# Nine of the sixteen input tiles come transposed from HBM instead of through TensorE, with a new list of operations

## The chip, the cores and the metric

The kernel runs on one core of one Trainium2 chip. The metric is the time of one execution on the device in microseconds (us); the lower the better. The kernel before takes 492.57 us, the median of three runs (491.83 to 493.06).

## The reference, cut to what matters

The input x has 2048 rows (tokens) of 512 numbers. It is normalised by rows, then goes through two branches, whose results are multiplied and added to x.

```python
x = A_x                                     # 1 x 2048 x 512
xn = _layernorm(x, axis=-1)                 # (x - mean) / sqrt(var + 1e-5), row by row
s = _A_ref(xn, A_wqkv, A_w_phi, A_wo)       # linear attention, 32 heads of 16
g = _silu(_B_ref(xn, B_w1, B_b1, B_w2))     # dense 512 -> 1792, mish, dense 1792 -> 512
return x + s * g

# in _A_ref: qkv = x @ wqkv; q and k go through w_phi and two softmaxes each;
# kv = phi_k^T v and z = sum of phi_k over all tokens; o = phi_q kv / (phi_q z); o @ wo
```

## The kernel before, in words

The 2048 tokens are 16 tiles of 128 tokens (`NT`), numbered 0 to 15. Every matrix product on TensorE needs the normalised x transposed: features on the partitions, tokens along the row. In the kernel that is `xT`, one tile of 128 x 2 x 4 x 128 for each 128 tokens: the first half (called high) is the value rounded to the fast matmul type fp32r, the second half (low) is what the rounding left. Each product then takes three matmuls (low by high, high by low, high by high), which `mm3` and `kv_product` issue.

The function `norm` (operation `N` in the list `ORDER`) makes one tile of `xT`. It loads the tile of x with tokens on the partitions (`load_x`), takes mean and variance by BN_STATS and BN_AGGR on VectorE (`mv`), computes one over the deviation (an addition on VectorE, a power on GpSimd, `rs`) and minus mean by that (`nb`), normalises the tile in one pass with these as scalars of each partition (on VectorE or ScalarE), and lets TensorE transpose it by four matmuls with the identity into a bank of PSUM (`pt`). `split` copies the bank out twice: ScalarE writes the high half, VectorE the low one. Then the tile goes to HBM (`scr`) for the second branch.

The products use Strassen's scheme with seven products in place of eight, so sums and differences of pairs of tiles are needed, here tile t and tile t + 4. `sums_x` makes them (`ts`, and split `th` and `tl`) from the two banks `pt`: since an instruction of GpSimd can't read PSUM here, it first copies one of the banks to SBUF (`xr`). They go to HBM too (`scrT`).

After that come, for the attention: products for k and v (`kv_a` to `kv_d`, banks `kx`, `ky`, `kz`), for q (`q_proj`, bank `q`, stored to HBM as `qd` from a copy `qs` and loaded again), two softmaxes each (`k_soft`, `q_soft`), the sums over all tokens (`kv_acc`, bank `kvp`; `sums`), denominators (`den`) and a transposition of each q tile in blocks into `ph0` (tiles 0 to 7) or `ph1` (8 to 15), the products with kv (`num`, banks `pn`, which need all eight tiles of `ph0` or `ph1`) and with wo (`att_out`). For the other branch: `ffn1a` to `ffn1d` (banks `fx`, `fy`, `fz`), the activation Mish, `ffn2` and `ffn2a` to `ffn2d`. `final` takes SiLU, multiplies by the attention's result and adds x, and stores.

No scheduler runs at build time that would decide the order. Every operation is recorded by `Program`, and a table of numbers, `SCHED`, says in which order the recorded operations are issued, and by a letter behind a number on which of two engines an operation runs where both could do it (V is VectorE, G GpSimd, A ScalarE). A second table, `PLACE`, gives each tile its place in the pools: 38 slots, 15 small slots `s2`, the banks of PSUM and some more. Each engine takes its instructions strictly in the order of the list, so an instruction that waits holds all that stand behind it on its engine. All DMAs but the very first are issued from SyncE (SP), also in order. Since all operations are issued by one helper, nearly all instructions have line 182 in the profile.

Of the kernel before, what the change touches and what calls it, by code (L numbers as in the profile page):

```python
# [10 lines left out]
F32 = mybir.dt.float32  # L11
# [19 lines left out]
PLAIN = (0,)  # L31
# [18 lines left out]
232A 275 236 380 233 193 210 92 325 183 110V 308 37 237 211 158 238 64 178 360 111G 220 184A 239 194 118A 125V 188G  # L50
179 167 195A 180 240A 276 361 168 427 212 93 112 259 196 391 213 241 169V 277 221 200A 381 362 146G 326 197 245A 214
327 65 278 127 309 279A 119 198 166 215A 201 223 246 242 260V 222A 247G 224 328 202V 428 310 203V 329 392 280 311 128A
249 429 330 227 243 284A 312 147 248V 225V 216 228A 254 285 319G 217 561 287V 84 161 382 113 255 286G 293 256A 363 288
331A 257 364 313 199 295 320 314V 218 281 393 162V 394 315 250 332 261 114 316 599 94 321G 159 294A 204 148 333 430
305 395 181 317 289 282 263 251V 306A 383 365A 396V 229 115G 322 307 262V 350 264 384 265 340 266 296 336 318 297 226
341 299G 252 366 185 342 337 267G 205 323A 268G 355 370A 351A 371 344V 431A 372G 352 298 367 338A 290V 300G 432 269
356 368 270 369 397 219 422 139 398 373V 374 401A 399 385A 324 436A 353A 357V 386 301 400 95V 459 358 207 437 387 170
334 420 438G 354 206G 375 388 410 440 423A 343 421A 404V 457 302 345G 474 402 376G 208 346 411 244 271 253 458A 507
335 460 412 519 461 403V 414V 472 405 413 447 462 415G 473A 303 475 463G 416 445 600V 272G 520A 439V 484 508A 477 441
389 347 377 525 339 602G 446V 464G 348 485 442V 349G 469 486A 448 465 476 509 417 433 406 478G 378 424 487 470A 407G  # L60
488 526A 505 471 466 495 489G 449 450 304G 522 496 408 291 510 521 451V 498 452G 549 497 527 490G 573 467 479V 491
562V 551 566 499V 564G 512 523A 651 539 500V 409 601G 292 434 501 492 468G 532 511 553 533A 493 513G 480 418 419V 591
494G 550A 552A 540 453 524 481 574 482 603G 565V 514G 611 542 575A 558 541 577 612A 543V 567V 578 544V 559V 693 506A
560 639 515 435 454 570G 572 545 638 637 455 528 579A 534 516 563G 640 618 685 456G 647 517 712 529 546 483G 502 581
646 530A 547 635 503 548G 582 571V 621 650 283 518G 649 535 583 613 536 531 504V 580 614 593V 576 622 594V 595 652V
584 598 623A 654V 713 636A 624 610 604 596V 443 554 605V 625 585V 656 653V 698 597V 615 537A 586V 555 657V 824 587
608V 568 645 620 648 643 556A 609G 616A 619V 557 680 854 714 538 588 444 660 655G 699V 606 569G 682 617 681A 661A 663
662 626 687 678 694G 658 686 664A 668 688G 679V 696G 707 607G 644 592V 665 669 589 627 709 689G 628 695V 702 715V 629V
641 716V 727 630G 642 671 717 666 720 697G 708A 659V 667 728A 778 722 721A 590V 700 739 631 683 701G 710 723 632 704
750G 792 724A 703V 684 690 633 670 733 725 672G 718 726 729 711 821 634V 736 673V 751G 756 730 674 734V 705 735 675  # L70
706 743 793G 731V 732 822 744A 676 691 677G 746 757 753V 752 747A 740A 759V 755 754G 834 856 829 766 831 741 780 767
797V 719 828 771 779 995 768A 764V 832 823 786 765V 745 692 802 781G 758 774 787A 748 788 769 742 849 830 803G 775 770
737 843 855 850A 794G 804 806 760G 846 807A 799 844V 782G 795 798 845 872 800 805V 801 796V 808 789 873A 888 835V 783
827 813G 749 862 790 833 761 836 777 867 863A 762 738 772A 837G 904 942 814 773 933 1037 905A 815V 816 817 877V 818G
874 838 784 819G 851 791 776 878 916 857G 847 896V 826 906 858G 986 763 885 897 879G 785 864 907 886A 852 859 880 898V
959 899 820 868A 917A 839 869 889 960A 840G 841G 865 920 900 918 881 919 875 923 882G 866 1039 853 876 901V 860 922
825 908G 912 902G 921A 861 1003 934A 997 924A 890 929 870 910G 977 943 925 883G 842 887 930A 1100 991 931 955 909V 932
992V 871 936 884 956A 913G 939 926 940 987G 811 903 1093 911G 941 963 961 891V 914 1089 935 962 1102 892G 809 937A 996
964A 1122 1006 944 988G 893 989V 927 982 950 915V 1087 928 1016 965 945V 978V 1099 946G 951V 810 952 848 957 983G 990V
1011 979G 966 1007 993 953 980G 1009 954 994V 981G 958 1045 967 1018 1088 1010A 969V 1017A 998G 1029 1101 970 1012  # L80
999G 1030A 1086 971V 1034 972 1013A 973 1019 1000 1014 1020 1031 968 1047 1008 974V 1123 938 975G 1032 1090 984 1001
947 1166 1097 1002 1021G 976 1053 1038 985V 1108 1054A 1033A 1055 1078G 1064 1109A 1022 1057 894 1065A 1094 1015 1046
1067 1058A 1040G 1096 1035 812 1004A 1079 1059 1041G 895 1095 1042 1060 1066 1048G 1133V 1023G 1114 1124 1125G 1484
1147 948 1080G 1049V 1164 1148A 1024 1115A 1025 1081 1043 1111 1103G 1165A 1185 1036 1061A 1050 1026G 1062 1141 1126G
1068 1027G 1051 1176 1092 1142A 1098 1167 1005 1149 1134 1082 1169 1112 1083G 1150 1119 1044 1151 1170A 1084V 1248
1135G 1144 1130 1104V 1056 1091 1028 1105 1172 1070G 1339 1177A 1085 1121 1173A 1127 1136 1145 1171 1249 1071 1190
1052 1137 1120A 1274 1072G 1138V 1073 1168 1174 1116 1139G 1220 1074 1357 1131 1191V 1152 1128 1485 1250 1140 1182
1340 1075V 1117 1076G 1179 1183 1106 1178 1180A 1257G 1153A 1181 1118 1197 1192 1194 1251 1154 1175 1143 1186 1107
1063 1132V 1358 1214 1200 1293 1198 1201 1188 1366 1156G 1204 1228 1392 1215A 1205 1155 1199 1276 1202 1193 1217 1208
949 1187G 1203 1445 1206 1225 1218 1252G 1195 1518 1207 1209 1146 1231 1229 1212 1226A 1157 1439 1359 1189G 1360 1275  # L90
1375 1254 1234 1235 1277G 1232 1238 1367 1255 1239 1216 1196G 1242 1221 1243 1459 1233 1253 1246 1258 1236 1320 1210
1278G 1256 1213 1247 1237 1158G 1227 1259V 1240 1341V 1265 1223 1260 1295 1279 1261 1159 1211 1262G 1224G 1077 1328
1266A 1241 1361G 1368 1129 1280 1281 1446 1268 1312G 1475 1377 1342 1321 1369 1294 1421 1343G 1313 1244 1344 1245
1222G 1334 1314V 1069 1407 1263V 1352 1362 1491 1269A 1345A 1323V 1346 1282V 1365 1430 1230 1296V 1301 1322 1270 1297V
1324G 1315 1160 1325 1290 1316 1161V 1317V 1162V 1335V 1298 1163 1363 1460 1355 1461 1408 1364 1356G 1264 1318G 1331
1326 1302A 1447 1303 1283 1395 1423 1370V 1409 1284G 1271 1336V 1304G 1353 1416 1113 1376 1291A 1371 1272V 1378 1292
1354V 1329A 1373 1396V 1330 1285 1452 1393 1605 1372 1410 1379V 1533 1432 1299 1374 1422 1419 1286 1383 1332A 1411V
1420G 1382 1454 1417 1287V 1402 1394V 1380 1288G 1431 1305 1337 1486 1381 1300 1497 1333 1306G 1273 1413 1307 1289
1424 1611 1219 1448 1184 1338V 1414 1110 1308 1477 1309V 1425V 1403 1415 1327 1405 1428 1476 1406V 1404V 1412 1418V
1433 1310V 1499 1426 1434G 1453 1384V 1498 1429 1478 1427 1479V 1436 1347 1802 1385 1440 1438 1519 1492 1311 1386G  # L100
1539 1435 1524 1449G 1441 1387 1480 1535 1520 1388 1482 1455 1389V 1319 1390G 1437 1462G 1391 1451 1463G 1442V 1450
# [93 lines left out]
def block_kernel(ctx: ExitStack, tc: tile.TileContext, x, xt, wqkT, wv, phi, wo, w1, b1, w2, out):  # L195
# [14 lines left out]
    def alloc(tag, shape, name, dtype=F32):  # L210
        return pools[tag].tile(shape, dtype, tag=tag + next(places), name=name)
# [687 lines left out]
```

## Time and profile before

| | |
|---|---|
| time, median of three runs | 492.57 us (491.83 to 493.06) |
| the profiled execution's own time | 492.47 us |
| its span (first to last instruction) | 490.7 us |
| mean granted clock of TensorE | 0.996 |
| transposes of x tiles on TensorE | 64, four for each tile |
| HBM traffic | 72.92 MB read, 42.07 MB written |

The profile is of one execution. PE is TensorE's matmul queue, PEld its loads of weights (they overlap), DVE is VectorE, ACT ScalarE, POOL GpSimd, SP SyncE and SPq its queue of DMA issues. A row of grouped instructions reads: line, engine, operation, names out<-in with buffer numbers left out, shapes, count; then busy time and mean duration in ns; then the idle time of the engine just before these instructions and what ended it. A row of waits reads: who waited <- for whom: us in total, times, longest. A row of a timeline reads: start, us from start to end, engine, line, operation, names, shapes, count.

### The profile page before, as it was taken

Reading aid. Unit: us, or ns where it says so; the run is one execution under the profiler, and the core shown is the slowest. Engines: PE = TensorE matmul, PEld = TensorE weight load, DVE = VectorE, ACT = ScalarE, POOL = GpSimd, SP = SyncE. Lnnn points to the kernel's source line nnn. Section 1 sums busy time; section 2 is a strip of 40 time slices with the busy share of each in tenths; the row PEclk is TensorE's granted clock in tenths of the full one; section 3 lists DMA queues with packets and bytes.
Section 4 is the critical chain, followed back from the end, with each engine's and each line's share of the span. In section 5 each row is a group of like instructions: output and inputs, shape, how many; then the busy total and the mean of one; then the engine's idle time right before and its main releaser. Section 6 shows DMA issues by size and latency. Waiting matters only on the chain.

```text
span 490.7 us, 8536 instructions
## 1 busy us (share of the span) xinstructions
PE 482.5 (98%) x3126; PEld 397.9 (81%) x3126; DVE 428.0 (87%) x658; ACT 270.1 (55%) x408; POOL 276.8 (56%) x204
## 2 busy tenths in 40 slices
PE   9999999999999999999999999999999999999994
PEld 9888888888888788887888778888888887888883
DVE  5998989999989998989999978979956699889974
ACT  4777754544071524333434778587496487657721
POOL 2889556986548657567575687353642334612440
PEclk9999999999999999999999999999999999999998
DMA  8736838344977689979788896867686652484366
GB/s 296 286 123 243 303 126 338 152 133 120 375 253 265 207 289 342 287 258 298 264 268 286 319 351 233 278 196 234 214 288 230 211 193 67 152 276 154 107 203 203
DMA packets 65592, 115.53 MB, mean 235 GB/s; under 512 B 7056, under 2 KB 32016, under 8 KB 65552
## 3 DMA queue, kind: packets, MB, share of 16 engines
q1 hardware_dynamic: 65408, 114.75, 68.6%
q8 instruction: 24, 0.39, 0.3%
q10 hardware_dynamic: 144, 0.26, 0.1%
q14 instruction: 16, 0.13, 0.1%
HBM read 72.92 MB, written 42.07 MB: 234 GB/s over the span
## 4 chain that ended last, share of the span: by engine, by line
PE 94%; DVE 3%; issue 1%; DMA 1%; POOL 0%; SPq 0%; ACT 0%; DVEq 0%; ACTq 0%
PE y L182 19%; PE fx L182 14%; PE q L182 9%; PE pw L182 9%; PE kx L182 8%; PE fy L182 8%; PE x L182 6%; PE ky L182 4%; PE fz L182 3%; PE pn L182 2%; PE kz L182 2%; PE z L182 2%; PE kvp L182 2%; PE pt L182 1%; PE k L182 1%; PE v L182 1%
## 5 line engine op out<-in xcount | busy, mean ns | idle before, releaser
L182 PE MATMUL q<-wqh,xT 128*128 128x512 f32 x128 | 43.0, 395 | 0.0
L182 ACT ACTIVATE r<-r,b1t 128x512 f32<-128x512 f32 x56 | 37.9, 715 | 3.0 <-DMA r<-hd 3.0
L182 PEld LDWEIGHTS q<-wqh,xT 128*128 128x128 f32 x128 | 24.0, 188 | 5.1
L182 PE MATMUL q<-wql,xT 128*128 128x512 f32 x64 | 25.0, 390 | 0.0
L182 DVE TENSOR_REDUCE tz<-ez 128x64 f32<-128x1024 f32 x16 | 19.3, 1204 | 1.3 <-POOL ez L182 1.3
L182 ACT ACTIVATE hb<-fx 128x512 f32<-128x512 f32 x13 | 7.5, 593 | 18.4 <-PE fx L182 18.4
L182 PE MATMUL kx<-wss,th 128*128 128x512 f32 x56 | 17.3, 390 | 0.0
L182 POOL TENSOR_TENSOR w2t<-w2t 128x256 f32<-128x256 f32 (+1 forms) x4 | 6.0, 1496 | 19.7 <-DVE w2t L182 12.9
L182 ACT ACTIVATE qs<-q 128x512 f32<-128x512 f32 x12 | 6.9, 595 | 17.9 <-PE kvp L182 10.0
L182 POOL TENSOR_TENSOR rs<-rs,mhalf 128x1 f32<-128x1 f32 x16 | 9.8, 620 | 12.0 <-DVE rs L182 11.3
L182 DVE TENSOR_TENSOR ol<-pn,oh 128x256 fp32r<-128x256 f32 x32 | 12.1, 415 | 4.9 <-ACT oh L182 4.9
L182 ACT ACTIVATE hc<-fx 128x512 f32<-128x512 f32 x13 | 7.7, 598 | 15.0 <-PE fx L182 15.0
L182 ACT ACT_TABLE_LOAD x12 | 15.4, 1283 | 0.2
L182 ACT ACTIVATE w1sh<-w1s 128x1024 fp32r<-128x1024 f32 x7 | 7.4, 1059 | 11.8 <-DVE w1s L182 6.2
L182 PEld LDWEIGHTS q<-wql,xT 128*128 128x128 f32 x64 | 12.0, 188 | 2.3
L182 DVE BATCH_NORM_STATS2 st<-x 128x6 f32<-128x512 f32 x16 | 10.7, 682 | 3.6 <-DMA x<-x 3.6
L182 POOL TENSOR_TENSOR w<-w2r,w 128x512 fp32r<-128x512 f32 x7 | 9.0, 1295 | 8.5 <-ACT w L182 8.5
L182 DVE TENSOR_TENSOR xT<-pt,xT 128x512 fp32r<-128x512 f32 x16 | 10.8, 680 | 2.0 <-ACT xT L182 1.2
L182 PE MATMUL pw<-oh,wo0l 128*128 128x512 f32 x32 | 12.5, 390 | 0.0
L182 PE MATMUL pw<-ol,wo0h 128*128 128x512 f32 x32 | 12.5, 389 | 0.0
L182 PE MATMUL pw<-oh,wo0h 128*128 128x512 f32 x32 | 12.5, 389 | 0.0
L182 PE MATMUL pw<-oh,wo1l 128*128 128x512 f32 x32 | 12.4, 389 | 0.0
(862 smaller groups left out, 1864.3 us busy)
## 6 DMA issues: line engine op xcount, KB each, us to landing
r<-hd SPq DMA_DIRECT2D x28, 512.0 KB, 5.3
qd<-qs SPq DMA_DIRECT2D x16, 256.0 KB, 6.3
scr<-xT SPq DMA_DIRECT2D x8, 512.0 KB, 5.3
scrT<-th SPq DMA_DIRECT2D x8, 512.0 KB, 4.6
scrT<-tl SPq DMA_DIRECT2D x8, 512.0 KB, 5.4
qp<-qd SPq DMA_DIRECT2D x16, 256.0 KB, 5.8
xx<-xt SPq DMA_DIRECT2D x16, 256.0 KB, 4.9
so<-so SPq DMA_DIRECT2D x16, 256.0 KB, 3.1
```

The source lines that it names most:

```text
L182: getattr(g, m)(*a, **k)
```

## The change

For the nine tiles in `TURNED` the host's transposed copy of x (`xt`, which `final` reads already) takes the place of the transposition on TensorE. The mean and the deviation of each token are computed as before from the tile with tokens on the partitions, which is still loaded. But now they are needed along the row, the same on all partitions. So the pair `mv` of each partition is written to HBM as two rows of 128 numbers (`row`, one number from each partition), and loaded back to all 128 partitions (`bc`). The transposed tile is loaded from `xt` (`nx`), the mean is subtracted and the product with one over the deviation taken, in two passes over 128x512 on VectorE or GpSimd. `nx` takes the place of `pt` behind that: in SBUF, so that its low half and its sums may also be made on GpSimd, and no copy `xr` is needed where the second tile of a pair is turned.

`norm_turned` is new, `norm` branches to it, the end of `norm` becomes `keep_x`, and `sums_x` takes either kind:

```diff
+TURNED = (3, 6, 7, 9, 10, 11, 13, 14, 15)
...
+    def norm_turned(t, mv):
+        rs = mv[:, 1:2]
+        V.tensor_scalar(rs, rs, 1e-5, None, op0=ALU.add)
+        G.tensor_tensor(rs, rs, mhalf, op=ALU.pow)
+        row = dram.tile([2, P], F32, name=f"row{t}")
+        Q.dma_start(row.rearrange("c p -> p c"), mv)
+        bc = alloc("s2", [P, 2, P], f"bc{t}")
+        Q.dma_start(bc.rearrange("p c n -> p (c n)"), row.rearrange("c n -> (c n)").partition_broadcast(P))
+        nx = alloc("s2", [P, KC, P], f"nx{t}")
+        Q.dma_start(nx, xt.rearrange("(k p) n -> p k n", p=P)[:, :, t * P:(t + 1) * P])
+        for c, op in ((0, ALU.subtract), (1, ALU.mult)):
+            either(nx, nx, bc[:, None, c, :].to_broadcast([P, KC, P]), op=op)
+        return nx
...
         V.bn_aggr(mv, st)
+        if t in TURNED:
+            w = slot([P, 2, KC, P], f"xT{t}", F32R)
+            pt = norm_turned(t, mv)
+            split(pt, w[:, 0], w[:, 1], either)
+            return keep_x(t, w, pt)
...
-        xr = s2(f"xr{t}")
-        copy(xr, p2.rearrange("p k n -> p (k n)"))
-        xr = xr.rearrange("p (k n) -> p k n", k=KC)
+        xr = p2
+        if p2.space == "PSUM":
+            xr = s2(f"xr{t}")
+            copy(xr, p2.rearrange("p k n -> p (k n)"))
+            xr = xr.rearrange("p (k n) -> p k n", k=KC)
+        first = V.tensor_tensor if p1.space == "PSUM" else either
...
-        V.tensor_tensor(ts[:, 0], xr[:, 0:2], p1[:, 0:2], op=ALU.subtract)
+        first(ts[:, 0], xr[:, 0:2], p1[:, 0:2], op=ALU.subtract)
```

`SCHED` and `PLACE` are replaced as a whole by other numbers; the list `ORDER`, by which the operations are recorded, stays as it is. The first line of `SCHED`:

```diff
-27 16 0 13 1 46 2 19 3 15 4 74 5 17 28 6 96 7 14 18 8 123 9 29 10 30 47 20 11 31 12 42 129 48 32 49 33V 50 120 21 51
+27 13 0 74 1 96 2 16 3 46 4 15 5 17 28 6 18 7 14 123 8 120 29 9 30 75 10 149 31 11 12 76 98 32 276 33V 129 47 42 99 48
```

What this does to the queues is shown at three places. The first is TensorE just ahead of the first product with tile 3 (bank `kx3`, from the high half of the k weights `wkh` and `xT3`). Before:

```order
L182 MATMUL kz2_309<-wkh1_176,xT2_231 128x512
L182 MATMUL kz2_309<-wkl1_177,xT2_231 128x512
L182 MATMUL kz2_309<-wkh1_176,xT2_231 128x512 x2
L182 MATMUL kz2_309<-wkl1_177,xT2_231 128x512
L182 MATMUL kz2_309<-wkh1_176,xT2_231 128x512
L182 MATMUL pt9_322<-ident_83,x9_316 128x128 x4
L182 MATMUL pt10_332<-ident_83,x10_326 128x128 x4
L182 MATMUL kx3_290<-wkh0_160,xT3_265 128x512
```

And in the changed kernel at the same place:

```order
L183 MATMUL v4_269<-wv1h_212,xT4_168 128x512
L183 MATMUL v4_269<-wv1l_213,xT4_168 128x512
L183 MATMUL v4_269<-wv1h_212,xT4_168 128x512 x2
L183 MATMUL v4_269<-wv1l_213,xT4_168 128x512
L183 MATMUL v4_269<-wv1h_212,xT4_168 128x512
L183 MATMUL kx3_289<-wkh0_160,xT3_264 128x512
```

The transposes of tiles 9 and 10 are gone, as are those of 3, 6 and 7 further ahead; products of tiles 4 and 8 stand there that came later before, and a product of tile 2 (`kz2`) comes behind.

The second place is SP's list of DMAs around the pair of rows of tile 3: `row3` is its write to HBM, `bc3` its load to all partitions. In the changed kernel (`scr` and `scrT` are stores of finished tiles, `qd1` is the store of tile 1 of q, `nx11` the transposed load of tile 11):

```order
L183 DMA qd1_109<-qs1_274 128x512
L183 DMA row9_318<-mv9_316 128x2x1
L183 DMA bc6_281<-row6_280 128x256
L183 DMA row3_265<-mv3_263 128x2x1
L183 DMA nx11_357<-xt 128x4x128
L183 DMA scr1_103<-xT5_220 128x2x256
L183 DMA scrT0_106<-tl0_174 128x1024
L183 DMA bc7_301<-row7_300 128x256
L183 DMA x14_358<-x 128x512
L183 DMA bc3_266<-row3_265 128x256
L183 DMA qd2_110<-qs2_238 128x512
```

Before, at the rows with these numbers, stand stores alone, the last of which is that of tile 12 of q:

```order
L182 DMA scrT0_106<-tl0_174 128x1024
L182 DMA qd4_112<-qs4_206 128x512
L182 DMA qd0_108<-qs0_236 128x512
L182 DMA scrT0_106<-th1_225 128x1024
L182 DMA w1a2_449<-w1 128x1024
L182 DMA scr0_102<-xT1_184 128x1024
L182 DMA qd12_120<-qs12_287 128x512
```

The loads of nine rows and nine transposed tiles now stand among these stores, and those of q come later.

The third place is VectorE around the transposition of tile 7 of q into `ph0`, the last that `num` needs. Before:

```order
L182 SCALAR_TENSOR_TENSOR den8_726<-tz8_725 128x32
L182 TENSOR_TENSOR hc6_784<-hc6_784,fy6_782 128x512
L182 RECIPROCAL den8_726<-den8_726 128x32
L182 COPY hc5_792<-fx5_769 128x512
L182 TENSOR_REDUCE q13s_761<-q13e_760 128x64
L182 STREAM_TRANSPOSE ph0_584<-q7e_710 128x32x32
```

In the changed kernel:

```order
L183 STREAM_TRANSPOSE ph0_579<-q6e_627 128x32x32
L183 TENSOR_REDUCE q11m_831<-qp11_829 128x32
L183 TENSOR_TENSOR q7e_705<-q7e_705,q7r_703 128x1024
L183 TENSOR_TENSOR hb6_778<-hb6_778,fy6_777 128x512
L183 STREAM_TRANSPOSE ph0_579<-q7e_705 128x32x32
L183 TENSOR_REDUCE tz8_720<-ez8_719 128x64
```

The scaling of `q7e` is now done by VectorE itself, two places ahead of its transposition, and the steps of the denominator of tile 8 have moved behind.

More of the change, by code (lines that the diff above doesn't have):

```diff
@@ L50 @@
[L50 to L59, printed above, removed]
@@ new lines @@
+196 282 165A 229 370 244G 180 200A 201 439 245G 390 93 168 230A 197 440 161 325V 225 441 169A 401 263V 215 112 127
+284G 170 166 202V 319 226 198 251V 371 203V 309 249 318 285G 217V 147 119 257 84 250V 218G 338 204 442 402 258 337
+162V 219 372 320G 205 472 252 391 220V 326 207 321G 297 408 253 113 148 246 223 392 254V 227A 322 128A 264 403 323V
+298A 247V 299 289V 265A 373 339V 290G 664 248 266 300 228 340G 301 231 292G 267 303G 341 114 404 259A 302 328 405 268
+304G 406 327V 344 255 329A 260 291G 310A 185 363 269 94 293 270G 407 364 311 181 393 305 271V 159 360 375V 272 294V
@@ new lines @@
+553 429 587 464G 356 484 452G 590 588A 505 613G 454 589 421 578G 508 448V 357G 554 536A 562 524 479 545 565A 455V 651
+518 465V 491G 509 591 571 526V 492V 537 527G 592A 506 466 593 307 456 624 480 507G 546A 296 467 493 400 548 563A 556V
+308G 510 604 494 549 605A 511 615G 457 614V 512G 631 430 555 659 616G 495 573 513V 576G 547 632A 585 572V 519A 625A
+566 528 557V 663 725 580V 594 514 583V 558 567 431V 581 584G 648 529 634 515 595 665G 656 635 652 559 606G 657 541
+636A 597 516 626 627 667G 481V 517G 568 847 650 468 413 560 628 596 530 561V 542 843 496V 608 543A 653 617 607V 611
@@ new lines @@
+669 623 550A 670V 629A 638 569A 609V 649A 698 570 531V 673 707V 658 619 720 469V 630 551 674A 660 610V 691 637 544 711
+633 618V 805 692A 449 621V 598G 695 726 693 712V 708G 639 676 694A 599V 709G 696 722 677A 675 668G 697 600 661 699
+728G 717 640 721A 622V 678 666V 836 727 620G 681 723 641 715 582V 662 769 729G 733 716A 679 671 682 680 740 834 701G
+700 734A 724 684 710G 736 672V 741A 642G 713 752 601 702G 743 683 753A 714V 737A 742 703 643V 685G 758 644 754 718
+744A 756 602 719 686V 755 603G 645 687 746 654 770 735 646 747A 763V 757A 647G 748 835 759 791 688 745 764V 765 655
@@ new lines @@
+1042 916 1046A 950A 983 1024 951 998G 1043A 1013 966 1025 1060 967 1014 1091G 1066 1026A 1137 1027 1070 1067A 1288
+1028 984G 1034G 822 1092 1077 1071A 1114 1073 907 958G 1106 1103 957 1160 941 1074A 908 1452 959G 1035 1109 1154 824
+1261 1015 985 1179 1036G 1155V 1078A 1053G 960 986 987V 1072 1037 988G 961 1127 1048 1110 1068 1093G 1121 1075 1038
+1076 1054V 1039G 1069 1177 1094 1055 823 1061G 989 1079 1157 1178A 1138V 1128A 1180 1124 1062V 1146V 1063 1129 1161A
+1125 1083G 1105 1262 1111 1056 1080 1130 1132 1122A 1147 1104 1139G 1112 1126 1064 1040G 1199 1182 1181 1133A 1263
@@ new lines @@
+1057 1162 1065 1183A 1095 1041 1189 1370 1116G 1148V 1131 1264 1096G 1185 1149 1200G 1163 1233 1388 1097V 1184 1117G
+1186A 1140 1192 1187 1158 1165 1150 1193A 1143 1290G 1098 1151G 1195 1289 1166A 1207 1164 1190A 1152V 1372 1203 1347
+1196 1379 1153 1134 1270G 1353 1081 1371 1191 1084 1118 1082 1265G 1167 1210 1271 1144 1204V 1389 1205 1230 1206 1333
+1213 1188 1241 1211 1194 1212 1208 1169G 1214 1049 1227 1215 1242 1217 1201 1231 1238 1085G 1202G 1228V 1266 1209G
+1216 1218 1219 1239A 1220 1244 1170 1221 1390 1306 1145G 1222 1488 1335 1240 962 1229 1267 1458 1247 1223 1248 1245
@@ new lines @@
+1224 1348G 1251 1246 1443 1225 1268 1252 1291G 1255 1236 1256 1325G 1269 1226 1249 1259 1260 1250 1341 1086 1253 1292
+1254 1272V 1307 1273 1308 1278 1334 1342A 1309V 1234 1489 1336V 1434 1472 1119 1337G 1504 1168 1357 1087 1618 1460
+1120 1343 1380 1326 1171G 1310G 1172 1355 1237G 1173 1281 1381 1257 1474 1258 1088V 1293 1284 1373 1420 1089V 1415
+1159 1358A 1374G 1090 1311 1314 1279V 1349V 1280 1354G 1282A 1274 1436 1356V 1283 1156 1235G 1686 1344 1429 1174V
+1285A 1243 1382 1531 1275V 1175V 1232 1350 1624 1378 1422 1351G 1312 1315A 1338 1375 1383V 1695 1365 1276V 1377 1444
@@ new lines @@
+1787 1840 1776V 1801 1863 1760V 1896 1828 1755 1738V 1802 1844 1829V 1739G 1805A 1874 1767V 1832 1763G 1856 1768V
+1803A 1764 1811V 1824 1806A 1765V 1769 1788G 1812V 1804A 1831 1833V 1868 1823 1740 1813 1789V 1836 1841V 1830 1790
+1741V 1880 1834 1797V 1864 1837V 1835 1877 1865V 1848 1839 1878V 1770V 1838 1875V 1902 1857V 1876 1862 1791V 1843 1703
+1845V 1842 1849V 1907 1846 1814V 1869V 1866G 1850 1921 1884 1847 1890 1854 1910 1852 1891 1889 1851 1881V 1885 1883
+1858 1853 1908V 1897 1861 1886V 1911 1898G 1855 1920 1892V 1870 1903 1901 1893V 1873 1887V 1899V 1888 1879 1867 1904V
@@ L123 @@
+1894 1882 1905V 1906 1900 1909 1930 1922 1931V 1916 1923V 1934 1932V 1926 1924V 1912 1933 1917V 1913V 1925 1918V 1914V
+1919 1935V 1915 1936V 1927V 1937 1928V 1929
 """
 PLACE = """
[20 rows of a table removed]
[20 rows of a table added]
 """
@@ L346, in norm, with keep_x @@
         split(pt, w[:, 0], w[:, 1])
+        keep_x(t, w, pt)
+    def keep_x(t, w, pt):
         xT[t], pts[t] = w, pt
@@ L365, in sums_x @@
             G.tensor_tensor(ts[:, 2], xr[:, 2:4], xr[:, 0:2], op=ALU.subtract)
-        V.tensor_tensor(ts[:, 3], p1[:, 2:4], ts[:, 1], op=ALU.subtract)
+        first(ts[:, 3], p1[:, 2:4], ts[:, 1], op=ALU.subtract)
         th, tl = (slot([P, 4, 2, P], f"t{n}{t}", F32R) for n in "hl")
```

109 lines of the change are left out of this document (41 added, 68 removed), and 40 rows, old and new, of the table PLACE.

## The prediction

> **What bounds the kernel now.** I read the page first: the busy row of each engine and the chain that ended last. In a busy row stand the engine, its busy time, its share of the span and the number of its instructions.
>
> ```profile
> PE 482.5 (98%) x3126; PEld 397.9 (81%) x3126; DVE 428.0 (87%) x658; ACT 270.1 (55%) x408; POOL 276.8 (56%) x204
> PE 94%; DVE 3%; issue 1%; DMA 1%; POOL 0%; SPq 0%; ACT 0%; DVEq 0%; ACTq 0%
> ```
>
> TensorE (PE) is busy for 482.5 of 490.7 us, and 94% of the chain runs through it. Busy need not mean fed, so I asked next for all the waits of PE, and then for three long stretches, whose columns are PE, PEld, DVE, ACT and POOL busy, the granted clock, DMA share and GB/s.
>
> ```profile
> PE wake L182 <- DVE mhalf L265: 1.1, 1, 1.1
> PE fy L182 <- DVE hc L182: 0.3, 1, 0.3
> PE fy L182 <- DVE ha L182: 0.3, 1, 0.3
> 20.00:140.00 120.00, 120.00 (x853) 99.57 (x852) 113.64 (x201) 65.12 (x96) 84.19 (x60) 1.00 0.59 211
> 140.00:280.00 140.00, 139.40 (x792) 114.52 (x791) 131.49 (x187) 58.51 (x85) 91.80 (x68) 1.00 0.84 278
> 280.00:490.70 210.70, 204.20 (x1362) 165.89 (x1360) 168.68 (x236) 134.92 (x210) 90.89 (x61) 0.99 0.63 211
> 479.73 4.47 PE L182 MATMUL x<-md,w 128*128 128x512 f32 x19
> ```
>
> PE waits 1.7 us in all. Its last matmul ends at 479.73 + 4.47 = 484.2, and 6.5 us of SiLU, products and stores follow. So the time is: the start, PE's own work at full clock, 0.6 us of waits, and the tail. Two things follow. PE work that goes shortens the run, and there is nearly no waiting left to win. VectorE (DVE) is the second limit: until 280 us it idles only 6.4 + 8.5 = 14.9 of 260 us.
>
> **What goes from PE.** A tile costs four transposes.
>
> ```profile
> L182 PE MATMUL pt<-ident,x 128*128 128x128 f32 x64 | 9.3, 272 | 0.0
> 44.50 0.60 PE L182 MATMUL pt<-ident,x 128*128 128x128 f32 x4
> 44.85 0.48 PE L182 MATMUL kx<-wss,tl 128*128 128x512 f32 x1
> 46.33 0.60 PE L182 MATMUL pt<-ident,x 128*128 128x128 f32 x4
> 54.49 0.39 PE L182 MATMUL kx<-wss,tl 128*128 128x512 f32 x1
> 55.85 0.39 PE L182 MATMUL kz<-wkh,xT 128*128 128x512 f32 x1
> ```
>
> The mean of 272 ns is how long one transpose is in flight; four together take 0.60 us, so they overlap. What they cost the queue is read from starts. From 44.50 to 46.33, 1.83 us, PE takes four transposes and six matmuls of 128x512; from 54.49 to 55.85, 1.36 us, it takes six such matmuls alone (0.227 each). So four transposes cost 0.47 us. The order lists 64 before and 28 after, all other matmuls in equal number: nine tiles by 0.47 is **4.2 us**. The Trainium skill, page "TensorE: Matmul & The Clock Gate", Part 4, gives about 275 ns for a transpose in one kernel's context; the trace has the same duration, 272 ns, and 36 of them in a row would be 9.9 us, an estimate from that page which the starts contradict here.
>
> **What is added on the elementwise engines.** A turned tile gets two passes over 128x512 (12 of the 18 on GpSimd (POOL), six on DVE), and ScalarE (ACT) and DVE or POOL split it from SBUF, not from a bank.
>
> ```profile
> L182 DVE TENSOR_SCALAR nb<-mv,rs 128x1 f32<-128x1 f32 x16 | 3.0, 202 | 0.6 <-POOL rs L182 0.4
> L182 DVE TENSOR_SCALAR x<-x,mv,rs 128x512 f32<-128x512 f32 x5 | 2.7, 538 | 0.0
> L182 DVE TENSOR_TENSOR xT<-pt,xT 128x512 fp32r<-128x512 f32 x16 | 10.8, 680 | 2.0 <-ACT xT L182 1.2 <-ACT xr L182 0.8
> L182 DVE TENSOR_TENSOR ts<-pt,ts 128x256 f32<-128x256 f32 x11 | 4.5, 406 | 0.0
> L182 DVE COPY qs<-q 128x512 f32<-128x512 f32 x4 | 2.7, 683 | 0.3 <-PE q L182 0.3
> L182 DVE TENSOR_TENSOR r<-r 128x512 f32<-128x512 f32 x7 | 5.8, 840 | 0.0
> L182 DVE TENSOR_TENSOR wss<-ws,wss 128x1024 fp32r<-128x1024 f32 x2 | 2.4, 1212 | 0.0
> L182 DVE TENSOR_TENSOR w1sl<-w1s,w1sh 128x1024 fp32r<-128x1024 f32 x4 | 5.7, 1413 | 0.2 <-PE fy L182 0.2
> L182 POOL TENSOR_TENSOR w<-w2r,w 128x512 fp32r<-128x512 f32 x7 | 9.0, 1295 | 8.5 <-ACT w L182 8.5
> ```
>
> I count DVE's rows up to the transposition of q7e, the eighth tile of `ph0` and what `num` waits for: 420 instructions before, 406 after. Out: nine `nb` (1.8), three normalisations (1.6), four `ts` (1.6), three `xT` (2.0), seven copies out of banks, net (4.8). In: six `nx` passes, for which no row of this shape with a broadcast operand stands; the nearest are 0.54 (one input) and 0.84 (two inputs in SBUF), and I take 0.68, nearer the second: 4.1. Also in, because the list moves whole passes of 128x1024 between the engines: 14 come to DVE (`tl`, `wss`, the scaling of k) and three leave, net 11 at 1.3, between 1.21 and 1.41: 14.3. Steps of q's softmax and of `den` that now stand behind q7e take off 4.7, small ones 0.2. Sum: 4.1 + 14.3 - 11.8 - 4.9 = **+1.7 us** on DVE to that point, 1 to 4 by the two ends of the prices. POOL gives up about as many long passes as it gets (12 `nx` and three `xT` at 1.3 against nine `tl`, `wss` and scalings at 2 to 3).
>
> **Where this meets PE.** In the timelines of PE and DVE:
>
> ```profile
> 53.03 0.48 PE L182 MATMUL kx<-wkh,xT 128*128 128x512 f32 x1
> 276.35 1.23 DVE L182 STREAM_TRANSPOSE ph<-q7e 128x1024 f32<-128x1024 f32 x1
> 280.67 2.76 PE L182 MATMUL pn<-ph,kvw 32*32 32x256 f32 x128
> DVE hb L182 <- PE fy L182: 2.7, 2, 1.8
> ...
> DVE w1sl L182 <- PE fy L182: 0.2, 1, 0.2
> ```
>
> q7e is done at 277.6 and `num` starts at 280.7: 3.1 us to spare. Ahead of `num` PE has 1103 matmuls of 128x512 in both orders, and only the 4.2 us are gone, so it arrives at 276.5. If DVE ran at its old waits it would be done at 279.3: PE waits **2.8 us**. But seven of the waits of DVE between 20 and 280 us end on PE, 6.4 us together (the first and the last row of them stand above), and these shrink when PE comes earlier; if 2.8 of the 6.4 go, the wait is nothing. I take a quarter, 0.7, since PE's other producers have more to spare.
>
> **The new chain of transfers.** A turned tile waits for its row to go to HBM and come back to all partitions; three DMAs a tile, 27 in all, at 0.4 us of SP's queue each. The first tile that is needed is x3. Ahead of `kx3` PE has 151 matmuls and 12 transposed tiles before, 157 and seven after: 53.03 + 6 x 0.227 - 5 x 0.47 = 52.0 us.
>
> ```profile
> 35.45 0.68 DVE L182 TENSOR_TENSOR xT<-pt,xT 128x512 fp32r<-128x512 f32 x1
> 37.77 1.06 POOL L182 TENSOR_TENSOR rs<-rs,mhalf 128x1 f32<-128x1 f32 x2
> 31.73 0.33 SPq L182 DMA_DIRECT2D qd<-qs  x1
> 39.47 1.42 SPq L182 DMA_DIRECT2D scr<-xT  x1
> 50.34 0.32 SPq L182 DMA_DIRECT2D qd<-qs  x1
> x<-x SPq DMA_DIRECT2D x15, 256.0 KB, 5.8
> kvw<-kvd SPq DMA_DIRECT2D x4, 128.0 KB, 5.4
> b1t<-b SPq DMA_DIRECT2D x1, 7.0 KB, 5.6
> L182 ACT ACTIVATE xT<-pt 128x512 fp32r<-128x512 f32 x16 | 9.6, 598 | 5.0 <-PE pt L182 4.5 <-DVE ts L182 0.5
> L182 ACT ACT_TABLE_LOAD x12 | 15.4, 1283 | 0.2
> ```
>
> After `bc3` has landed x3 needs 0.68 + 1.3 + 0.60 + 0.68 = 3.3 us, so it must land by 48.7. `row3` has its numbers once the deviation of x3 is through, the 73rd row of DVE and the 31st of POOL; the rows of these places ran at 35.45 and 37.77 before (the first two above; in the new list less of DVE's and POOL's long work stands ahead of them). So the numbers are there by 35 to 38, and two trips of at most 5.6 and 5.4 us end by 46 to 49: in time at the first, 0.3 us late at the second. I take no cost. No row shows a row write of 256 single numbers; `b1t`, 1792 single numbers, is the nearest and no slower than the whole tile of x. The Trainium skill, page "DMA: Bandwidth & Descriptors", Rules for kernel authors, speaks against this write: a strided last dimension lowers to one descriptor per element. By that rule the second rival below gains; the row of `b1t` bounds it at 5.6 us.
>
> ACT loads tables 19 times in the list, not 13 as before: 7.7 us more of an engine that is 55% busy; hidden beside PE, 1.3 us if one falls ahead of a bank that PE waits for. Tail: the last pieces of `final` stand in the same order. Both at 0.
>
> **Sum.** The profiled execution took 492.47 (span 490.7, 1.8 around it), 0.1 under the median. 492.57 - 4.2 + 0.7 = **489.0 us** (rounded down), with 487.6 (no wait at `num`, and the two waits of 0.3 gone too) to 490.2 as this case's own range.
>
> **Rivals.**
> First, DVE takes the gain: the wait at `num` is the whole 2.8 us or DVE lags as much elsewhere. For it: 95% busy, and 1.7 us more in front of that point. Against: 6.4 us of its idle time end on PE. Time: 492.6 - 4.2 + 2.8 = 491.2, on the edge of what a measurement tells from no change, 0.3% or 1.5 us.
> Second, slower: `bc3` comes late. SP takes its DMAs in order, and in the trace it stood still from 40.9 to 50.3 us, until a `qs` was copied. Held so with `bc3` still queued, it would issue at 50.3 and land at 53 to 56, x3 would be ready at 56 to 59 and `kx3` start 4 to 7 us late, with x6, x9 and `tl2` close behind. At the middle: 492.6 - 4.2 + 6 = 494.4. It loses from a delay of 4.2 us on, `bc3` landing after 52.9. Against it: `bc3` stands ahead of the late `qd` issues in SP's list, behind a single `qs`, that of tile 1, which went out at 32 us in the trace.
> Third, a transpose costs its whole 272 ns: 36 of them are 9.8 us, 483 us. The starts in the timeline speak against it.
>
> **Chances.** Forecast 0.58, first rival 0.20, second 0.16, third 0.02, the rest (a wait of another kind) 0.04. The range 487.6 to 492.6 leaves out the second and third, 0.18. Faster by over 0.3%, below 491.1: the forecast, the third and half of the first, 0.70. Within: the other half and a little of the rest, 0.12. Slower: 0.18.
>
> **What would show it.** PE busy down by about 4 us to 478; 28 transposes; `kx3` starting near 52 with no wait in front; at `num` a wait of PE on DVE between 0 and 2.8; 6.5 us after the last matmul. Wrong if the waits of PE grow by more than 3 us, if one of them ends on `xT3` or on a DMA, or if PE's busy time falls by much more than 4 us.

## The result and the profile after

The changed kernel takes 527.28 us (median of four runs, 525.46 to 529.86), the kernel before 492.28 us beside it (median of four, 491.83 to 493.06). The ratio is 1.071 (95% interval 1.065 to 1.077): slower by 7%, or 35 us. The prediction was 489.0 us, and faster; it was wrong.

The page of the changed kernel has the same rows as those shown of before: busy time of the engines, and the chain that ended last, by engine and by line.

```profile
PE 489.5 (93%) x3090; PEld 398.7 (76%) x3090; DVE 430.2 (82%) x639; ACT 275.9 (53%) x411; POOL 291.4 (56%) x221
PE 76%; DMA 16%; DVE 4%; POOL 3%; issue 1%; SPq 0%; ACT 0%; DVEq 0%; POOLq 0%; ACTq 0%
```

PE has 36 instructions fewer, as the change says, and yet its share of the span went from 98 to 93%. The chain went through DMA for 1% of the span; now it is 16%. The second question is where, and three views answer it. The waits of PE (total, times, longest):

```profile
PE kx L183 <- DVE ts L183: 6.8, 1, 6.8
PE kz L183 <- DVE ts L183: 5.7, 1, 5.7
PE ky L183 <- DVE kp L183: 4.1, 2, 3.8
PE kx L183 <- DVE v L183: 3.9, 1, 3.9
PE ky L183 <- ACT kp L183: 2.5, 1, 2.5
PE kz L183 <- DVE kp L183: 1.7, 1, 1.7
PE kx L183 <- ACT qs L183: 1.4, 1, 1.4
```

Together 26.1 us. None ends on a DMA directly: `ts` are sums of tiles, one of which is turned, and its producer waited in turn. The table of stretches (PE, PEld, DVE, ACT, POOL busy, granted clock, DMA share, GB/s) shows that all of it lies in one region, 20 to 130 us, where PE is idle for 110.00 - 84.02 = 26.0 us:

```profile
40.00:50.00 10.00, 8.34 (x37) 6.53 (x35) 2.95 (x4) 2.30 (x3) 0.00 (x0) 1.00 1.26 69
50.00:60.00 10.00, 2.90 (x6) 1.82 (x6) 1.09 (x3) 0.00 (x0) 3.61 (x4) 0.83 0.87 120
60.00:70.00 10.00, 6.31 (x20) 5.06 (x21) 8.61 (x12) 5.54 (x9) 9.18 (x7) 0.66 1.32 263
20.00:130.00 110.00, 84.02 (x336) 65.44 (x336) 70.81 (x123) 43.17 (x65) 55.02 (x48) 0.91 0.93 185
```

Read the first row from the right. The DMA engines are occupied on average for more than the whole stretch (a share over 1 means that packets overlap), but move 69 GB/s; before, the stretch from 20 to 140 us ran at 211 GB/s with a share of 0.59. DVE, ACT and POOL have nearly run out of work, POOL entirely, and PE follows in the second row. So transfers are under way, and slow. From 130 us on PE is full again. The timeline has `num` here:

```profile
312.63 2.76 PE L183 MATMUL pn<-ph,kvw 32*32 32x256 f32 x128
```

That is 32.0 us later than before (280.67), so of the 33.0 us by which the span grew (490.7 to 523.7) nearly all are lost ahead of it. The list of DMA issues (count, KB each, median us to landing) names the slow ones:

```profile
x<-x SPq DMA_DIRECT2D x15, 256.0 KB, 6.4
nx<-xt SPq DMA_DIRECT2D x9, 256.0 KB, 10.4
bc<-row SPq DMA_DIRECT2D x9, 128.0 KB, 6.1
row<-mv SPq DMA_DIRECT2D x9, 1.0 KB, 13.2
```

The smallest transfer of the kernel, 1 KB, takes longest. In SP's timeline around tile 3, with the order of the list known, the rows are `bc6`, `row3`, `nx11`, a store, a store, `bc7`, `x14` and `bc3`:

```profile
37.06 0.33 SPq L183 DMA_DIRECT2D bc<-row  x1
37.49 0.64 SPq L183 DMA_DIRECT2D row<-mv  x1
38.18 0.46 SPq L183 DMA_DIRECT2D nx<-xt  x1
38.69 0.50 SPq L183 DMA_DIRECT2D scr<-xT  x1
41.44 0.33 SPq L183 DMA_DIRECT2D scrT<-tl  x1
45.40 0.33 SPq L183 DMA_DIRECT2D bc<-row  x1
50.15 0.33 SPq L183 DMA_DIRECT2D x<-x  x1
55.26 0.32 SPq L183 DMA_DIRECT2D bc<-row  x1
```

`row3` was issued at 37.5 us, inside the 35 to 38 us that the prediction gave for its numbers. That is luck: the numbers were there by 32.5 us, when GpSimd had ended the fifth of its powers for turned tiles (five rows are issued up to here), and SP's list stood at `bc6` until an earlier row write, issued at 26.38, had landed at 37.05. The chain that ended last has the trips of these two rows as one piece each (start, us):

```profile
26.38 10.67 DMA row<-mv
37.49 17.68 DMA row<-mv
```

`row3` landed 17.68 us after its issue, and only then, at 55.26, could `bc3` go. VectorE's pass on `nx3` started only when `bc3` was there, the sums behind it in VectorE's list came after it, and PE's wait of 6.8 us for them ended at 63.7. The timelines have the pass, and `kx3` twelve matmuls after the one that waited:

```profile
61.39 1.57 DVE L183 TENSOR_TENSOR nx<-nx,bc 128x512 f32<-128x512 f32 x1 [7.20 <-DMA bc<-row]
68.20 0.39 PE L183 MATMUL kx<-wkh,xT 128*128 128x512 f32 x1
```

`kx3` started at 68.2 us where 52.0 was expected. The numbers of the row were early; the trips of the rows, an earlier one's first and then its own, were long.

### The profile page after: what moved, and what is told of

It is laid out like the page before. It is cut to its first block, busy times and chain, and to the rows that moved or that the text cites. A ratio compares the mean times of both kernels' runs of the same rounds, so it can differ in the third digit from the quotient of the medians.

```text
span 523.7 us, 8498 instructions
## 1 busy us (share of the span) xinstructions
PE 489.5 (93%) x3090; PEld 398.7 (76%) x3090; DVE 430.2 (82%) x639; ACT 275.9 (53%) x411; POOL 291.4 (56%) x221
## 4 chain that ended last, share of the span: by engine, by line
PE 76%; DMA 16%; DVE 4%; POOL 3%; issue 1%; SPq 0%; ACT 0%; DVEq 0%; POOLq 0%; ACTq 0%
PE y L183 18%; PE fx L183 15%; DMA row<-mv 10%; PE pw L183 8%; PE fy L183 7%; PE x L183 7%; PE q L183 4%; PE fz L183 4%; DMA bc<-row 3%; PE kx L183 3%; PE ky L183 2%; PE pn L183 2%; PE z L183 2%; PE kvp L183 1%; DMA qd<-qs 1%; DMA scrT<-tl 1%
## 5 line engine op out<-in xcount | busy, mean ns | idle before, releaser
L183 POOL TENSOR_TENSOR nx<-nx,bc 128x512 f32<-128x512 f32 x12 | 18.0, 1506 | 33.2 <-DMA bc<-row 27.3
L183 ACT ACTIVATE xT<-nx 128x512 fp32r<-128x512 f32 x9 | 5.6, 625 | 29.1 <-POOL nx L183 29.1
L183 DVE TENSOR_TENSOR nx<-nx,bc 128x512 f32<-128x512 f32 x6 | 6.0, 993 | 17.8 <-DMA bc<-row 17.8
L183 PE MATMUL kx<-wkh,xT 128*128 128x512 f32 x28 | 11.1, 438 | 8.2 <-DVE ts L183 6.8
L183 PE MATMUL kz<-wkh,xT 128*128 128x512 f32 x28 | 10.8, 433 | 7.4 <-DVE ts L183 5.7
L183 ACT ACTIVATE kp<-kx 128x512 f32<-128x512 f32 x14 | 8.2, 597 | 16.4 <-DVE xT L183 4.8
L183 POOL TENSOR_TENSOR ts<-nx,ts 128x256 f32<-128x256 f32 x7 | 6.6, 941 | 17.8 <-DVE ts L183 13.2
L183 PEld LDWEIGHTS kx<-wkh,xT 128*128 128x128 f32 x28 | 5.8, 207 | 10.5 <-DVE ts L183 7.5
L183 POOL TENSOR_TENSOR w<-w2r,w 128x512 fp32r<-128x512 f32 x8 | 11.5, 1438 | 3.7 <-ACT w L183 3.7
L183 PEld LDWEIGHTS kx<-wss,th 128*128 128x128 f32 x56 | 11.3, 201 | 2.8
```

What stands on the lines that cost most here:

```text
L183: getattr(g, m)(*a, **k)
```

## The experiments

### Which part of the new chain is slow

Three theories: A, the write of 256 single numbers is slow and holds up the transfers beside it; B, only its reader's wait in SP's list in order is at fault; C, the new reads are. Four runs on one chip tell them apart. First, no write:

```diff
-        Q.dma_start(row.rearrange("c p -> p c"), mv)
...
-        Q.dma_start(bc.rearrange("p c n -> p (c n)"), row.rearrange("c n -> (c n)").partition_broadcast(P))
+        Q.dma_start(bc.rearrange("p c n -> p (c n)"), x[t * P, 0:2 * P].partition_broadcast(P))
```

> The nine row writes are left out, and bc is loaded from 256 numbers of x, so the tiles are normalised by wrong numbers; all else is the changed kernel. Three theories. A: the write of 256 single numbers is itself slow (13.2 us to landing at the median) and holds up the transfers that are under way beside it. B: the write is slow only because it is one more trip in SyncE's list in order, where its reader holds all that stands behind it (SP waited 40.3 us on row writes in six places). C: the reads are at fault, the transposed load in pieces of 512 B (10.4 us to landing) and the load of 1 KB to 128 partitions. A and B both expect 488 to 492 us here, nx back to about 6 us to landing, and PE waits of 1 to 3 us. C expects 510 us or more, with nx still at 9 us or more.

Measured: 490.93 us (490.64 to 491.85), ratio to before 0.997 (0.996 to 0.998). All its waits of PE:

```profile
PE wake L185 <- DVE mhalf L268: 1.1, 1, 1.1
PE kz L185 <- DVE kp L185: 0.5, 1, 0.5
```

And two rows of its DMA issues:

```profile
nx<-xt SPq DMA_DIRECT2D x9, 256.0 KB, 5.6
bc<-x SPq DMA_DIRECT2D x9, 128.0 KB, 5.0
```

The whole loss is gone, and nx lands in 5.6 us in place of 10.4. The new list, the reads in pieces of 512 B and the passes on `nx` are all still there, so C falls. Second, the write is made, but nobody reads it:

```diff
         Q.dma_start(row.rearrange("c p -> p c"), mv)
...
+        Q.dma_start(bc.rearrange("p c n -> p (c n)"), x[t * P, 0:2 * P].partition_broadcast(P))
```

> The row writes are made as in the changed kernel, but nothing reads them: bc is loaded from 256 numbers of x, so the tiles are normalised by wrong numbers. A expects the transfers beside the writes still late (nx and x at 8 us or more to landing) and the time between, 500 to 520 us, since only SP's 40 us of waits go. B expects 488 to 492 us and nx near 6 us, since nobody waits for the slow trip. C expects 510 us or more, the same as without the writes.

Measured: 514.41 us (509.91 to 515.84), ratio 1.043 (1.038 to 1.048). Its DMA issues:

```profile
nx<-xt SPq DMA_DIRECT2D x9, 256.0 KB, 8.6
bc<-x SPq DMA_DIRECT2D x9, 128.0 KB, 8.1
row<-mv SPq DMA_DIRECT2D x9, 1.0 KB, 10.2
```

And the wait of SP's queue on these writes:

```profile
SPq L183 <- DMA row<-mv: 11.0, 5, 3.8
```

B falls. `bc` reads a row of the input here that is there from the start, and still takes 8.1 us in place of 5.0. The tiles of x, which A expected late as well, were not (6.5 us; 6.7 without the writes). SP's 11.0 us of waits on row writes are not for data, since nobody reads it. In the trace SP's DMAs count on eight semaphores in turn, and each waits for the one before it on its own: the first `bc` here went out at 36.53 us, when the eighth DMA ahead of it, a row write issued at 26.30, had landed. So a slow write holds the list even if nobody reads it. But the transfers themselves are slower too: in the trace's packets between 20 and 130 us one of 512 B, of which `nx` is made, took 45 ns on average, and 28 in the run without writes. So nine writes of 1 KB cost 514.4 - 490.9 = 23.5 us with nobody reading them, by what they do to the transfers beside and behind them, and the remaining 527.3 - 514.4 = 12.9 us, by this difference, come from waiting for their data. Third, the whole computation with the pair of each partition in one piece of 8 B:

```diff
-        row = dram.tile([2, P], F32, name=f"row{t}")
-        Q.dma_start(row.rearrange("c p -> p c"), mv)
-        bc = alloc("s2", [P, 2, P], f"bc{t}")
+        row = dram.tile([P, 2], F32, name=f"row{t}")
+        Q.dma_start(row, mv)
+        bc = alloc("s2", [P, P, 2], f"bc{t}")
...
-            either(nx, nx, bc[:, None, c, :].to_broadcast([P, KC, P]), op=op)
+            either(nx, nx, bc[:, None, :, c].to_broadcast([P, KC, P]), op=op)
```

> The whole computation, with the pair of mean and deviation kept together: each partition writes 8 B in one piece, 128 pieces a tile in place of 256, and bc holds the two interleaved. A expects about half the loss of 35 us, 500 to 512 us, with the row write at 5 to 8 us to landing. B expects 520 us or more while the trip is as slow as other small ones; C expects no change, 525 us.

Measured: 500.94 us (500.80 to 503.20), ratio 1.017 (1.015 to 1.019). The issue of its row:

```profile
row<-mv SPq DMA_DIRECT2D x9, 1.0 KB, 7.4
```

Half the pieces, eight of them in each 64 B in place of sixteen, the same bytes, the same trip: 10 us of loss are left of 36, less than the half that A expected, though inside its range. Fourth, eight pieces of 128 B, with every wait in its place (a few columns of `wide` are set to zero first):

```diff
-        mv = alloc("st", [P, 2], f"mv{t}")
+        wide = alloc("st", [P, 32], f"mv{t}")
+        mv = wide[:, 0:2]
...
-        Q.dma_start(row.rearrange("c p -> p c"), mv)
+        Q.dma_start(row.rearrange("c (a n) -> (c a) n", n=32), wide[0:8, :])
```

> The write of a row has the same 1 KB, the same place in SP's list, the same wait for the deviation and the same reader waiting for it, but goes out as eight pieces of 128 B from eight partitions (of which only the first columns hold a mean and a deviation, so the tiles are normalised by wrong numbers). A expects the row write at 2 to 4 us to landing, no transfer beside it late, and 488 to 493 us. B expects the trip and its waits to stay, 510 us or more. C expects 510 us or more.

Measured: 490.16 us (489.61 to 490.23), ratio 0.995 (0.993 to 0.996). The list of DMA issues gives no time to landing for these nine writes. SP's timeline bounds that of `row3`, since `bc3` (the second row) waits for it:

```profile
32.98 0.32 SPq L183 DMA_DIRECT2D row<-mv  x1
37.07 0.32 SPq L183 DMA_DIRECT2D bc<-row  x1
```

At most 4.1 us, where it took 17.7; 2 to 4 were expected.

The timelines of PE and DVE give the places of which the prediction spoke, `kx3`, the transposition of q7e and `num`:

```profile
51.91 0.39 PE L183 MATMUL kx<-wkh,xT 128*128 128x512 f32 x1
274.07 1.23 DVE L183 STREAM_TRANSPOSE ph<-q7e 128x1024 f32<-128x1024 f32 x1
277.40 2.76 PE L183 MATMUL pn<-ph,kvw 32*32 32x256 f32 x128
```

The round trip through HBM stays, with its reader waiting; at this speed it costs nothing. A's forecasts of the time hold in all four runs.

### The same writes in the kernel before

```diff
-        Q.dma_start(scr[g][:, i], f32(w)[:, :, g % 2 * 2:])
+        with one():
+            Q.dma_start(scr[g][:, i], f32(w)[:, :, g % 2 * 2:])
+            if t in (3, 6, 7, 9, 10, 11, 13, 14, 15):
+                row = dram.tile([2, P], F32, name=f"row{t}")
+                Q.dma_start(row.rearrange("c p -> p c"), f32(w)[:, 0, 0, 0:2])
```

> The kernel before, whole, with nine more DMAs: behind the store scr of each of the nine tiles a write of 256 single numbers to a row in HBM, which nobody reads. If the write is the cost by itself: clearly slower, 498 to 515 us, with x, qd and kx's tiles late. If it hurts only because of the new list, which has less slack in front of its transfers: 492 to 495 us.

Measured: 508.97 us (508.21 to 512.12), ratio 1.034 (1.031 to 1.037). Two rows of its DMA issues:

```profile
qd<-qs SPq DMA_DIRECT2D x16, 256.0 KB, 9.6
row<-xT SPq DMA_DIRECT2D x9, 1.0 KB, 13.3
```

And the longest wait of its PE:

```profile
PE kz L182 <- ACT v L182: 9.9, 1, 9.9
```

Nine writes that nobody needs, and the old list loses 16 us too. The x tiles, which I had expected late, were not (5.4 us, 5.8 before); the stores of q were (6.3 before).

### Why the write is slow

The write has many pieces, pieces of 4 B, pieces that lie side by side in HBM, and SP's queue. Each of these is taken away alone; all but the last run start from the kernel in which nobody waits for the rows (514.4 us). Reads of as many pieces of 4 B, in place of the writes:

```diff
-        Q.dma_start(row.rearrange("c p -> p c"), mv)
+        Q.dma_start(got[:, TURNED.index(t)], b1[0:2 * P].rearrange("(c p) -> p c", c=2))
```

> As the run in which nobody waits for the row writes, but in place of each write stands a read of 256 single numbers from HBM to two columns of SBUF (of b1, so nothing is computed from it; bc is again loaded from x, so the tiles are normalised by wrong numbers). If pieces of 4 B as such are slow, their count in the sixteen DMA engines: 510 us or more. If only writing them to HBM is: 490 to 493 us, with nx near 6 us to landing.

Measured: 490.60 us (490.05 to 491.08), ratio 0.996 (0.994 to 0.997). The issue of these reads:

```profile
got<-b SPq DMA_DIRECT2D x9, 1.0 KB, 4.3
```

When they are read, as many pieces cost nothing. Writes of 4 B with a distance between them (512 B here; 16 and 8 in place of the last P for the two runs that follow):

```diff
-        row = dram.tile([2, P], F32, name=f"row{t}")
-        Q.dma_start(row.rearrange("c p -> p c"), mv)
+        row = dram.tile([2, P, P], F32, name=f"row{t}")
+        Q.dma_start(row[:, :, 0].rearrange("c p -> p c"), mv)
```

> As the run in which nobody waits for the row writes (514.4 us), but each of the 256 numbers goes to its own place in HBM, 512 B from the next, in place of 4 B. Two theories of why the write holds up its neighbours. H1, one place in HBM: numbers that lie side by side are written one behind the other, since each needs the same line of memory; spread out they cost nothing: 490 to 493 us. H2, every small write costs the same wherever it goes: 510 to 518 us.

> As the run with the numbers 512 B apart (490.5 us; side by side 514.4), now 64 B apart; nobody reads the rows. If numbers hold each other up only within one 64 B of memory: 490 to 493 us. If within a stretch of 512 B, in which eight of them now lie: about as side by side, 505 us or more. If the loss grows with the number that share a stretch of 512 B: between, 494 to 505 us.

> As the run before this, with 32 B from one number to the next. If the stretch is 64 B, two numbers share it: a small loss, 491 to 497 us. If it is 32 B: 490 to 492 us, the same as with 64 B between them. If it is 512 B: 505 us or more.

Each run is held against the kernel before on its own chip:

| from one number to the next | us | ratio to before (95%) | row write to landing, median us |
|---|---|---|---|
| 512 B | 490.51 | 0.995 (0.994 to 0.997) | 4.4 |
| 64 B | 490.36 | 0.996 (0.994 to 0.997) | 4.1 |
| 32 B | 492.26 | 0.999 (0.998 to 1.000) | 4.9 |
| 4 B | 514.41 | 1.043 (1.038 to 1.048) | 10.2 |

The same 256 pieces of 4 B cost nothing that the time shows at 64 B apart, about 1.9 us in the whole kernel with two in each 64 B, and 24 us with sixteen. The row of the run at 64 B, to be held against that of the changed kernel:

```profile
row<-mv SPq DMA_DIRECT2D x9, 1.0 KB, 4.1
```

So it is neither the size of a piece nor the number of them, but how many are written close together in HBM. That the stretch which they must not share is 64 B is the simplest reading, and fits the pieces of 128 B, which lie side by side at no cost; distances between 32 and 64 B were not run. The Trainium skill, page "DMA: Bandwidth & Descriptors", Specifications, says that below 512 B the DMA does a read-modify-write. The runs put its cost more narrowly: pieces of 4 B, 64 B apart, are far below 512 B and cost nothing here; closer ones do. That one piece's reading and writing back of the 64 B has to end before the next one's starts would explain it, but this was not shown, only the distance at which the cost ends.

Last, the changed kernel with the writes on ScalarE's queue:

```diff
-        Q.dma_start(row.rearrange("c p -> p c"), mv)
+        A.dma_start(row.rearrange("c p -> p c"), mv)
```

> The changed kernel whole, with the nine row writes issued by ScalarE on its own queue in place of SyncE's. If the writes hold up the others in memory, past the queues: the time stays, 515 to 532 us, with nx and x as late as in the changed kernel. If they hold up what stands behind them in SyncE's queue: most of the loss goes, 500 us or less.

Measured: 524.69 us (523.84 to 526.11), ratio 1.065 (1.063 to 1.068). Two rows of its DMA issues:

```profile
nx<-xt SPq DMA_DIRECT2D x9, 256.0 KB, 12.3
row<-mv ACTq DMA_DIRECT2D x9, 1.0 KB, 11.7
```

`nx`, on SP's queue, is held up by writes on another as it was by those on its own. The time alone would not tell: with the writes in its list ScalarE is held up as well, and PE waits 11.0 us for a `qs` that ScalarE copies late. The Trainium skill, same page, "Issuing engines are not separate DMA queues", says that DMAs of all issuing engines run on the same 16 engines and interleave; this run agrees.

### A version without the slow write

Eight pieces of 128 B with the right numbers in them: the mean and one over the deviation stand in columns 0 and 16 of a block of 32, and VectorE's transposition by blocks of 32x32 puts each block's 32 means and 32 deviations into one partition each. The transposition stands in the list at the place of the row write; `wide` is set to zero once at the start.

```diff
-        G.tensor_tensor(rs, rs, mhalf, op=ALU.pow)
-        row = dram.tile([2, P], F32, name=f"row{t}")
-        Q.dma_start(row.rearrange("c p -> p c"), mv)
+        G.tensor_tensor(mv[:, 16:17], rs, mhalf, op=ALU.pow)
+        row = dram.tile([8, 32], F32, name=f"row{t}")
+        turned = turn[:, TURNED.index(t) % 4]
+        V.transpose(turned, mv)
+        Q.dma_start(row, turned[0:P:16])
...
-            either(nx, nx, bc[:, None, c, :].to_broadcast([P, KC, P]), op=op)
+            n4 = nx.rearrange("p k (b n) -> p k b n", n=32)
+            either(n4, n4, bc[:, None, :, c, :].to_broadcast([P, KC, 4, 32]), op=op)
```

> The whole computation, with the row made of eight pieces of 128 B: mean and one over the deviation go to columns 0 and 16 of a block of 32, VectorE transposes the 32x32 blocks (one small instruction a tile, at the place of the row write in the list), and eight partitions write 32 numbers each. If the small pieces of the write were the whole loss, as in the run with eight pieces: 489.5 to 491.5 us, faster than the kernel before by 0.2 to 0.6%, the row write at 4 to 5 us to landing and no wait of TensorE on xT, ts or kp above 1 us. If the nine added transpositions hold VectorE, which is busy nearly all the time there: 491.5 to 494 us.

Measured: 491.12 us (490.38 to 491.89), ratio to before 0.997 (0.996 to 0.998): 0.3% faster than the kernel before, and 7% faster than the changed one. The busy row of its page:

```profile
PE 480.6 (98%) x3090; PEld 393.7 (80%) x3090; DVE 432.3 (88%) x648; ACT 275.9 (56%) x411; POOL 295.3 (60%) x222
```

Its waits of PE where the loss was (those of the changed kernel there came to 26.1 us):

```profile
PE kz L183 <- DVE kp L183: 0.5, 1, 0.5
PE ky L183 <- DVE kp L183: 0.4, 1, 0.4
```

The groups of the two passes on `nx`:

```profile
L183 POOL TENSOR_TENSOR nx<-nx,bc 128x512 f32<-128x512 f32 x12 | 18.3, 1535 | 8.6 <-DMA bc<-row 7.0 <-DVE nx L183 1.4
L183 DVE TENSOR_TENSOR nx<-nx,bc 128x512 f32<-128x512 f32 x6 | 5.1, 844 | 0.7 <-DMA bc<-row 0.7
```

And the added transpositions, from the view of their tile (ns at the least, the median and the most):

```profile
L183 DVE STREAM_TRANSPOSE turn<-wide x9: 193/203/211, 26.2 to 63.7; 128x32 f32<-128x32 f32 x9
```

Nine transpositions of 0.2 us, with the pieces of 128 B that they make possible, remove 36 us. POOL still waits 7.0 us for `bc`, but has that time to spare.

## Why the prediction was wrong

The step that failed is "two trips of at most 5.6 and 5.4 us end by 46 to 49", from "No row shows a row write of 256 single numbers; `b1t`, 1792 single numbers, is the nearest and no slower than the whole tile of x". `b1t` is a read from HBM. The run with reads of 256 single numbers confirms that row: 4.3 us to landing. What had to be priced is a write whose numbers lie side by side, and that took 17.7 us for `row3`. The upper end of the cost came from a row that was near in the size of its pieces and on the wrong side of the transfer. The second error sits in the same sentence: the write was costed as latency of its own tile alone. Two thirds of the loss, 23.5 of 36.4 us, are there when nobody waits for its data: it is what the writes do to other transfers.

The second rival, `bc3` late, had the place and the sign: `bc3` went out at 55.26 us, where it thought of 50.3, and landed past the 52.9 from which it loses. Its reason was another (a `qs` that SP waits for), and its price of 494.4 us counted the delay of one tile, while nine writes came one upon another. The trigger and the size were the write's.

With the write out of the way the other steps can be read, in the run with eight pieces (490.16 us) and in the full version (491.12 us), both in the range of 487.6 to 492.6, the wider of the two that the prediction gives.
- `kx3` near 52.0: it started at 51.9 and 52.1.
- At `num`, where the forecast kept 0.7 us of wait, there is none: q7e was done at 274.07 + 1.23 = 275.3, `num` started at 277.4, so VectorE was not late. The first rival is out: of its 2.8 us of waits for VectorE the full version has 0.9, elsewhere (for `kp`). That this version takes nearly the rival's 491.2 us is luck.
- 4.2 us off PE: mis-sized. PE's busy time fell from 482.5 to 479.9 and 480.6, by 2.6 and 1.9 us, not by 4, and `num` came 3.3 and 2.1 us earlier (277.40 and 278.59 us in the timelines). Ahead of `num` PE had 3.1 and 2.4 us less to do; the 0.47 us for four transposes came from one place, and spread over nine tiles it was 0.34 and 0.26.
- Behind `num` and in the tail, put at nothing: from `num` on PE is busy for 204.1 and 204.0 us, where the same matmuls took 203.5 before, and 6.9 us follow its last matmul where 6.5 were forecast. Why, no run here tells.
- `nx` at 0.68 us on VectorE: 0.69 at the median in the full version; one of the six took 1.5, which makes the mean of 0.84. On POOL 1.4 at the median and 1.5 on average, for 1.3.

The lower end of the range is 0.2 us too low by its own terms (492.57 - 4.2 - 0.6 = 487.8); nothing hangs on it. The full version, 491.12, lies above the forecast's own upper end of 490.2.

So the gain of the nine tiles without that write is 1.7 to 2.4 us, each against the kernel before on its own chip, where 3.6 was forecast, and the 35 us come from one kind of transfer.

The price of a late tile was also larger than the wait. In the changed kernel, behind the wait of 5.7 us, PE's timeline and the table of stretches show:

```profile
54.57 0.63 PE L183 MATMUL kz<-wkl,xT 128*128 128x512 f32 x1
54.99 1.05 PE L183 MATMUL kz<-wkh,xT 128*128 128x512 f32 x2
54.00:57.00 3.00, 2.90 (x6) 1.79 (x6) 0.19 (x1) 0.00 (x0) 0.00 (x0) 0.50 0.82 148
```

A matmul starts 0.42 us after the one before it, where the prediction's rows had 0.227: the granted clock, the third number from the right in the last row, is 0.50 from 54 to 57 us, and 0.66 on average from 60 to 70. `num` is 32.0 us late although PE has about 3 us less to do ahead of it, 35 together; the waits are 26.1 of these. The other 9 I put down to the clock: the same 3090 instructions keep PE busy for 489.5 us here and for 480.6 in the full version, 8.9 longer. No run tested the clock alone.

## What to carry to other kernels

Before a few numbers per partition go to HBM, look at what lies side by side at the destination: if small pieces of one transfer are written less than 64 B apart, turn them on the chip first (a transposition by blocks of 32x32 took 0.2 us) or set them 64 B apart. Such a write is to be priced by all the transfers around it and not by its own bytes, and in the run that put it on another queue that didn't shield them. In the profile here it shows as DMA engines that are full at a low rate (1.26 of a share at 69 GB/s) and in loads that come late although nothing about them was changed. When a cost is bounded by the nearest row, that row must go in the same direction.

## What was not expected of the hardware

- Writes of 4 B that lie close together in HBM: 10.2 us to landing at the median with sixteen numbers in each 64 B, 4.9 with two, 4.1 with one; all with 256 pieces a transfer and nobody waiting.
- Their effect on others, with sixteen in each 64 B: a load of 1 KB to 128 partitions 8.1 us in place of 5.0, a load of 256 KB in pieces of 512 B 8.6 in place of 5.6.
- 256 reads of 4 B from HBM beside the same traffic: 4.3 us to landing, and no effect on the time.
